# One block of 64-wide products a pair in place of two, set inside a unit of the MLP

## The chip, the core and the metric

The kernel runs on one core of a Trainium2 chip, in one launch. The core has a matrix engine (TensorE, PE in the profile; its weight loads are listed apart as PEld), three engines for elementwise work (VectorE or DVE, ScalarE or ACT, GpSimd or POOL) and a queue for transfers (SP). Products land in PSUM, a small accumulator memory of eight banks; each bank holds 512 fp32 numbers in each of 128 partitions. The metric is the device time of one execution in microseconds, smaller is better.

## The reference

Eight batches of eight heads go through retention (causal attention without softmax, with a decay of its own for each head), and the 4608 rows of 512 that come out go through an MLP with a leaky activation. All is fp32.

```python
# B, H, S, D = 8, 8, 576, 64;  d_model = 512, d_ff = 2048
scores = (q @ k.transpose(0, 1, 3, 2)) / sqrt(D)
gamma  = 1 - 2.0 ** (-5 - arange(H))
rel    = arange(S)[:, None] - arange(S)[None, :]
Dmat   = where(rel >= 0, gamma[:, None, None] ** rel, 0)
attn   = (scores * Dmat) @ v
x      = attn.transpose(0, 2, 1, 3).reshape(B * S, H * D)
h      = x @ w_in
out    = (max(h, 0) + alpha * min(h, 0)) @ w_out
```

## The kernel before

**Retention.** Two heads make a pair, so that a batch has four pairs and the whole 32. A sequence is cut into nine chunks of 64. Within a chunk the masked scores are used as they are; what came before a chunk comes in through running sums of k^T v, one 64x64 matrix a chunk, decayed from chunk to chunk. For a pair this takes three blocks of small products on TensorE: `ps` (scores of k and q in each chunk), `pu` (k^T v of each of the first eight chunks), and `pv` (values: scores times v and sums times q, in one product each).

```python
def pair_scores(n, kT, qT):                       # mt: masked scores and q, side by side
    ps = [ps_tile([P, NM, C], ...) for p2 in range(2)]        # two banks
    for j in range(NJ):                                        # nine chunks, two heads
        for h2 in range(2):
            x = (1 - h2, h2)[j % 2]
            nc.tensor.matmul(ps[j % 2][half(x), j // 2], kT[half(h2), chunk(j)],
                             qT[half(h2), chunk(j)], start=True, stop=True)
    for h2 in range(2):
        nc.scalar.copy(mt[half(h2), h2]..., qT[half(h2)])
    for p2 in range(2):                                        # four masks
        for h2 in range(2):
            nc.vector.scalar_tensor_tensor(out=mt[to, h2, p2::2], in0=ps[p2][half(x), 0:nm], ...)
    return mt

def pair_states(n, kn, vn):                       # su: running sums
    ps = [ps_tile([P, NM - 1, D], ...) for p2 in range(2)]    # two banks
    for j in range(NJ - 1):
        for h2 in range(2):
            nc.tensor.matmul(ps[j % 2][half(x), j // 2], kn[half(1 - h2), j],
                             vn[half(1 - h2), h2, j], start=True, stop=True)
    nc.scalar.copy(su[:, 0::2], ps[0])
    for h2 in range(2):
        nc.vector.scalar_tensor_tensor(out=su[half(h2), 1::2], ...)    # 2
    for j in range(3, NJ - 1, 2):
        nc.vector.scalar_tensor_tensor(out=su[:, j], ...)              # 3, each on the one before
    nc.vector.scalar_tensor_tensor(out=su[:, 2::2], ...)               # 1
    return su
def pair_sums(vn, su):                            # the sums go beside v
    for h2 in range(2):
        nc.scalar.copy(vn[half(h2), h2, 1:], su[half(h2)])
# ... pair_values(n, vn, mt): products of vn and mt into two banks, copied to xb
```

Each fp32 product in the code is two instructions on TensorE in the profile: 18 score products are 36 instructions, 16 of k^T v are 32. All these small products take their banks from one pool, `ps_a`, which has two.

**The MLP.** Rows are taken in token blocks of 256, and the work on one is cut into eight units. Both matrix products are done with seven products of half the size in place of eight; sums and differences make up for it. A unit computes 14 products into two banks `ph[0]` and `ph[1]` (three and four quarters of a bank; the fourth quarter of `ph[0]` is not used), brings them to `g` with ScalarE and VectorE, and hands `g` to the output products `po` of seven half-wide results in four banks. The output products of a unit are issued one unit later. After the eighth unit's output products, one ScalarE copy and seven sums on VectorE empty `po`. Banks are held once: `ph` of the next unit waits until this one's is read, and `po` of the next token block until the last one is emptied.

```python
def mlp_unit(kb, i):
    ph = [ps_h.tile([P, 4, P], ...) for m in range(2)]
    for n, (m, o, l, r) in enumerate(...):                     # 14 products (28 instructions)
        for cc in range(2):
            nc.tensor.matmul(ph[m][:, o], w_in[...][:, l, ...], r[:, cc], ...)
    nc.scalar.copy(g[:, 7], ph[0][:, 2])
    for o, x0, x1 in (...):                                    # 4 sums that read ph
        nc.vector.tensor_tensor(out=o, in0=x0, in1=x1, op=ALU.add)
    # ... then 2 tensor_scalar, 1 scalar_tensor_tensor and 4 tensor_tensor on g alone
    pend.append((kb, i, g))
    if len(pend) > 1:
        mlp_out()                                              # 7 products of the unit before;
                                                               # after unit 7: out_block (empties po)
```

**How both are laced.** From the third batch on (24 pairs), the units that are ready are shared out over a batch's four pairs, four to a pair in most batches, and each block of small products stands between two units:

```python
share = -(-len(queue) // (NPAIR - c))
cuts = [(share + i) // 3 for i in range(3)][::-1]
mt = pair_scores(n, kT, qT)                  # block ps
pop_units(cuts[0])
pair_sums(vn, pair_states(n, kn, vn))        # block pu
pop_units(cuts[1])
# ... scale and transpose the next pair's k and q
pair_values(n, vn, mt)                       # block pv
pop_units(cuts[2])
```

Instructions are put in order on each engine when the program is built: what is written first goes first, and where the next one would have to wait, a later one may be set ahead of it.

Of the kernel before, what the change touches and what calls it, by code (L numbers as in the profile page):

```python
# [10 lines left out]
FP32 = mybir.dt.float32  # L11
# [3 lines left out]
ALU = mybir.AluOpType  # L15
# [3 lines left out]
def kernel(  # L19
# [10 lines left out]
    nc = tc.nc  # L30
    B, H, S, D = q.shape
    NTOK, DM = out.shape
    DFF = moe_w_in.shape[1]
    P = 128

    NPAIR = H // 2
    C = 64
    NJ = S // C
    NM = (NJ + 1) // 2
# [21 lines left out]
    attn = ctx.enter_context(tc.tile_pool(name="attn", bufs=1))  # L61
# [5 lines left out]
    pairs = [(b, c) for b in range(B) for c in range(NPAIR)]  # L67

    def half(x):
        return slice(x * C, (x + 1) * C)  # L70
# [113 lines left out]
    mask = const.tile([P, C], FP32, name="mask")  # L184
# [262 lines left out]
                          (t[:, 2], b21, t[:, 1])):  # L447
            nc.gpsimd.tensor_tensor(out=o, in0=x0, in1=x1, op=ALU.subtract)  # L448

    def mlp_unit(kb, i):  # L450
        if kb not in xt:
            combine_x(kb)
        x, t = xb[kb], xt[kb]
        ph = [ps_h.tile([P, 4, P], FP32, tag=f"psh{m}", name=f"ph{m}_{kb}_{i}")
              for m in range(2)]

        for n, (m, o, l, r) in enumerate((
                (0, 2, 0, x[:, 0:2, 0:P]), (0, 0, 2, x[:, 2:4, 0:P]), (0, 1, 5, t[:, 1]),
                (1, 0, 4, t[:, 0]), (1, 1, 1, x[:, 0:2, P:TB]),
                (1, 2, 6, x[:, 2:4, P:TB]), (1, 3, 3, t[:, 2]))):  # L460
            for cc in range(2):
                nc.tensor.matmul(ph[m][:, o], w_in[i // UST][:, l, i % UST, cc], r[:, cc],  # L462
                                 start=(n in (0, 3) and cc == 0), stop=(n in (2, 6) and cc == 1),
                                 skip_group_check=True)


        g = mlp.tile([P, 8, P], FP32, tag="g", name=f"g_{kb}_{i}")
        nc.scalar.copy(g[:, 7], ph[0][:, 2])  # L468
        for o, x0, x1 in ((g[:, 0:5:4], ph[0][:, 0:2], g[:, 7:8].to_broadcast([P, 2, P])),
                          (g[:, 5:7], ph[1][:, 0:2], g[:, 4:5].to_broadcast([P, 2, P])),  # L470
                          (g[:, 3], ph[1][:, 0], g[:, 6]),
                          (g[:, 1:3], ph[1][:, 2:4], g[:, 5:7])):
            nc.vector.tensor_tensor(out=o, in0=x0, in1=x1, op=ALU.add)  # L473
        for m in range(2):
            fc = m * NU + i
            nc.vector.tensor_scalar(g[:, 4 + 2 * m:6 + 2 * m], g[:, 2 * m:2 * m + 2], 0.0,  # L476
                                    alpha[:, fc:fc + 1], ALU.min, ALU.mult)
        nc.vector.scalar_tensor_tensor(  # L478
            out=g[:, 0:4].rearrange("p x t -> p (x t)"),
            in0=g[:, 0:4].rearrange("p x t -> p (x t)"), scalar=0.0,  # L480
            in1=g[:, 4:8].rearrange("p x t -> p (x t)"), op0=ALU.max, op1=ALU.add)
        for o, x0, x1, op in ((4, 1, 3, ALU.add), (6, 0, 1, ALU.subtract),
                              (5, 4, 0, ALU.subtract), (7, 2, 5, ALU.subtract)):
            ins = nc.vector.tensor_tensor(out=g[:, o, :], in0=g[:, x0, :], in1=g[:, x1, :], op=op)  # L484

        combine(3, ins)
        assert i < NU - UST or not waiting
        pend.append((kb, i, g))
        if len(pend) > 1:
            mlp_out()  # L490
# [11 lines left out]
            if ready[kb] == b:  # L502
                queue.extend((kb, i) for i in range(NU))

    def pop_units(n):
        for _ in range(min(n, len(queue))):
            kb, i = queue.pop(0)
            mlp_unit(kb, i)
            if i == NU // 2 and kb + 1 < NKB and ready[kb + 1] <= done[0]:
                combine_x(kb + 1)  # L510

# [4 lines left out]
    def ps_tile(shape, name):  # L516
        return ps_a.tile(shape, FP32, tag="psa", name=name)
# [19 lines left out]
    def chunk(j):  # L537
        return slice(j * C, (j + 1) * C)
# [3 lines left out]
    def pair_scores(n, kT, qT):  # L542
        c = pairs[n][1]

        mt = attn.tile([P, 2 * S], FP32, tag="at", name=f"mt_{n}").rearrange(
            "p (h j s) -> p h j s", h=2, s=C)
        ps = [ps_tile([P, NM, C], f"ps{p2}_{n}") for p2 in range(2)]
        for j in range(NJ):
# [5 lines that stand above are left out]
            nc.scalar.copy(mt[half(h2), h2].rearrange("p j s -> p (j s)"), qT[half(h2)])  # L554
        for p2 in range(2):
            for h2 in range(2):
                h, to, x = 2 * c + h2, half(1 - h2), (1 - h2, h2)[p2]
                nm = NM - p2
                nc.vector.scalar_tensor_tensor(  # L559
                    out=mt[to, h2, p2::2], in0=ps[p2][half(x), 0:nm], scalar=th[to, 3, h:h + 1],  # L560
                    in1=mask[to, None, :].to_broadcast([C, nm, C]), op0=ALU.mult, op1=ALU.mult)
        return mt

    def pair_states(n, kn, vn):
        c = pairs[n][1]
        ps = [ps_tile([P, NM - 1, D], f"pu{p2}_{n}") for p2 in range(2)]
        for j in range(NJ - 1):
            for h2 in range(2):
                x = (h2, 1 - h2)[j % 2]
                nc.tensor.matmul(ps[j % 2][half(x), j // 2], kn[half(1 - h2), j],  # L570
                                 vn[half(1 - h2), h2, j], start=True, stop=True)
        su = attn.tile([P, S], FP32, tag="kT", name=f"su_{n}")[:, 0:S - D].rearrange(
            "p (j d) -> p j d", d=D)
        g1, g2 = gch[:, 0, c:c + 1], gch[:, 1, c:c + 1]
        nc.scalar.copy(su[:, 0::2], ps[0])
        for h2 in range(2):
            nc.vector.scalar_tensor_tensor(
                out=su[half(h2), 1::2], in0=su[half(h2), 0::2], scalar=g1[half(h2)],
                in1=ps[1][half(1 - h2)], op0=ALU.mult, op1=ALU.add)
        for j in range(3, NJ - 1, 2):  # L580
            nc.vector.scalar_tensor_tensor(out=su[:, j], in0=su[:, j - 2], scalar=g2,
                                           in1=su[:, j], op0=ALU.mult, op1=ALU.add)
        nc.vector.scalar_tensor_tensor(out=su[:, 2::2], in0=su[:, 1:NJ - 3:2], scalar=g1,  # L583
                                       in1=ps[0][:, 1:], op0=ALU.mult, op1=ALU.add)
        return su

    def pair_sums(vn, su):
        for h2 in range(2):
            nc.scalar.copy(vn[half(h2), h2, 1:], su[half(h2)])  # L589

    def pair_values(n, vn, mt):
        b, c = pairs[n]
        w = TB // C

        j1 = -b * NJ % w or w
        j1 += w if NJ - j1 > 6 else 0
        pv = [ps_tile([P, (j1, NJ - j1)[i], C], f"pv{i}_{n}") for i in range(2)]
        for j in range(NJ):
            for h2 in range(2):
                nc.tensor.matmul(pv[j >= j1][half(h2), j - (j1 if j >= j1 else 0)],  # L600
                                 vn[:, h2, j], mt[:, h2, j], start=True, stop=True)
        j = 0
        while j < NJ:
            kb, o = divmod(b * NJ + j, w)
            if kb not in xb:
                xb[kb] = ring.tile([P, NCC, TB], FP32, tag=f"x{kb % NRING}", name=f"xb_{kb}")
            m, i = min(w - o, NJ - j), j >= j1
            j0 = j - (j1 if i else 0)
            nc.scalar.copy(xb[kb][:, c, o * C:(o + m) * C].rearrange("p (j s) -> p j s", s=C),  # L609
                           pv[i][:, j0:j0 + m])  # L610
            j += m
# [274 lines left out]
    for n, (b, c) in enumerate(pairs):  # L886
        if n <= last:
            continue
        if n == last + 1:
            pop_units(1)  # L890
        if n + 1 < len(pairs) and n + 1 not in loaded:
            loaded[n + 1] = load_pair(n + 1)
        kn, _, _, vn = loaded[n]
        share = -(-len(queue) // (NPAIR - c))
        cuts = [(share + i) // 3 for i in range(3)][::-1]
        kT, qT = turned.pop(n)
        mt = pair_scores(n, kT, qT)
        pop_units(cuts[0])
        pair_sums(vn, pair_states(n, kn, vn))
        pop_units(cuts[1])  # L900
        if n + 1 < len(pairs):
            scale_pair(n + 1)
            turned[n + 1] = transposes(n + 1)
        pair_values(n, vn, mt)
        del loaded[n]
        pop_units(cuts[2])
        if c == NPAIR - 1:
            enqueue(b)
    pop_units(len(queue))
# [30 lines left out]
```

## Time and profile before

The time is 1026.29 us, the median of three runs (1025.18 to 1026.33).

| what | busy us | from |
|---|---|---|
| whole span | 1024.7 | head of the page |
| MLP units, first products (L462) | 277.8 + 213.4 | groups |
| MLP units, output products (L382) | 407.8 | groups |
| `pv` (L600), `ps` (L551), `pu` (L570) | 35.5, 22.3, 19.5 | groups |
| VectorE in all | 768.8 | engines |
| ScalarE in all | 267.5 | engines |
| transfers | 64.30 MB | DMA queues |

A group is named by its line in the kernel, its engine and what it writes and reads; "mean ns" is one instruction. Instructions of TensorE overlap, so a busy time of 218 ns for a small product says nothing of the step from one to the next; that is read from the starts in the trace. The chain of work that ended last lists, in order of time, on which instructions the end of the program hung: start, length, engine, name, line, number. A timeline lists all instructions of one engine, with the idle time ahead of them and who ended it in brackets.

### The profile page before, as it was taken

Reading aid. Unit: us, or ns where it says so; the run is one execution under the profiler, and the core shown is the slowest. Engines: PE = TensorE matmul, PEld = TensorE weight load, DVE = VectorE, ACT = ScalarE, POOL = GpSimd, SP = SyncE. Lnnn points to the kernel's source line nnn. Section 1 sums busy time; section 2 is a strip of 40 time slices with the busy share of each in tenths; the row PEclk is TensorE's granted clock in tenths of the full one; section 3 lists DMA queues with packets and bytes.
Section 4 is the critical chain, followed back from the end, with each engine's and each line's share of the span. In section 5 each row is a group of like instructions: output and inputs, shape, how many; then the busy total and the mean of one; then the engine's idle time right before and its main releaser. Section 6 shows DMA issues by size and latency. Waiting matters only on the chain.

```text
span 1024.7 us, 23101 instructions
## 1 busy us (share of the span) xinstructions
PE 1007.9 (98%) x9385; PEld 891.0 (87%) x9385; DVE 768.8 (75%) x2041; ACT 267.5 (26%) x599; POOL 176.7 (17%) x198
## 2 busy tenths in 40 slices
PE   6899999999999999999999999999999999999998
PEld 5666668999999999999999999999999999999997
DVE  7669967777878787776868787877787776667665
ACT  4556652223222222022122222222222211000000
POOL 4656675200200010100010000200020001010000
PEclk9999999999999999999999999999999999999999
DMA  9975744223223222112113222222222100000000
GB/s 237 234 195 146 184 75 97 46 59 59 62 42 67 49 46 57 24 45 45 41 31 67 47 52 46 63 46 59 48 47 57 24 22 2 22 1 21 1 21 22
DMA packets 229308, 64.30 MB, mean 63 GB/s; under 512 B 214337, under 2 KB 222545, under 8 KB 229201
## 3 DMA queue, kind: packets, MB, share of 16 engines
q1 hardware_dynamic: 227088, 62.29, 26.8%
q8 instruction: 74, 1.21, 0.5%
q10 hardware_dynamic: 2112, 0.53, 0.3%
q14 instruction: 34, 0.27, 0.1%
HBM read 53.35 MB, written 9.44 MB: 61 GB/s over the span
## 4 chain that ended last, share of the span: by engine, by line
PE 97%; DVE 1%; DMA 1%; ACT 0%; issue 0%; POOL 0%; ACTq 0%; DVEq 0%; POOLq 0%
PE ph L462 40%; PE po L382 38%; PE po L397 6%; PE ph L418 5%; PE pv L600 3%; PE ps L551 2%; PE pu L570 2%; DMA w_out<-in_q_dram 1%; PE pv L717 0%; PE pv L706 0%; PE ps L660 0%; DVE w_out L690 0%; PE pt L641 0%; DVE wc L308 0%; DVE pa L667 0%
## 5 line engine op out<-in xcount | busy, mean ns | idle before, releaser
L382 PE MATMUL po<-w_out,g 128*128 128x256 f32 x1792 | 407.8, 379 | 0.0
L382 PEld LDWEIGHTS po<-w_out,g 128*128 128x128 f32 x1792 | 331.1, 190 | 39.4
L473 DVE TENSOR_TENSOR g<-ph,g 128x256 f32<-128x256 f32 (+1 forms) x512 | 187.5, 387 | 184.9 <-ACT g L468 112.7
L462 PE MATMUL ph<-xb,w_in 128*128 128x128 f32 x2048 | 277.8, 279 | 0.0
L462 PEld LDWEIGHTS ph<-xb,w_in 128*128 128x128 f32 x2048 | 253.2, 192 | 8.1 <-issue 0.5
L462 PE MATMUL ph<-xt,w_in 128*128 128x128 f32 x1536 | 213.4, 275 | 0.0
L462 PEld LDWEIGHTS ph<-xt,w_in 128*128 128x128 f32 x1536 | 192.1, 192 | 0.0
L468 ACT COPY g<-ph 128x128 f32<-128x128 f32 x128 | 33.9, 265 | 395.7 <-PE ph L462 375.6
L484 DVE TENSOR_TENSOR g<-g 128x128 f32<-128x128 f32 x512 | 126.8, 289 | 7.8
L478 DVE SCALAR_TENSOR_TENSOR g<-g 128x512 f32<-128x512 f32 x128 | 91.7, 717 | 3.9
L476 DVE TENSOR_SCALAR g<-g,alpha 128x256 f32<-128x256 f32 x256 | 85.0, 374 | 3.7
L523 POOL TENSOR_TENSOR qx<-qx,tabx 128x576 f32<-128x576 f32 x28 | 32.7, 1167 | 310.9 <-DMA qx<-in_q_dram 255.0
L418 PE MATMUL ph<-xb,w_in 128*128 128x256 f32 x256 | 60.2, 390 | 1.4 <-ACT xb L724 1.4
L559 DVE SCALAR_TENSOR_TENSOR mt<-ps,th,mask 64x320 f32<-64x320 f32 (+1 forms) x112 | 57.8, 516 | 4.5 <-PE ps L551 2.7
L397 PE MATMUL po<-w_out,g 128*128 128x512 f32 x128 | 58.5, 599 | 0.9 <-DVE g L434 0.9
L418 PEld LDWEIGHTS ph<-xb,w_in 128*128 128x128 f32 x256 | 49.1, 195 | 11.1 <-issue 2.4
L448 POOL TENSOR_TENSOR xt<-xb 128x256 f32<-128x256 f32 x16 | 11.6, 726 | 214.4 <-PE ph L462 202.1
L448 POOL TENSOR_TENSOR xt<-xb,xt 128x256 f32<-128x256 f32 x32 | 23.6, 738 | 142.4 <-ACT xb L609 141.7
L528 ACT ACTIVATE vn<-vn,tabv 64x576 f32<-64x576 f32 x56 | 43.3, 773 | 16.2 <-DMA vn<-in_v_dram 15.7
L397 PEld LDWEIGHTS po<-w_out,g 128*128 128x128 f32 x128 | 23.5, 190 | 24.9 <-issue 22.5
L589 ACT COPY vn<-su 64x512 f32<-64x512 f32 x56 | 34.5, 616 | 37.5 <-DVE su L583 36.8
L609 ACT COPY xb<-pv 128x256 f32<-128x256 f32 (+3 forms) x84 | 22.6, 321 | 79.1 <-PE pv L600 79.1
(120 smaller groups left out, 687.0 us busy)
## 6 DMA issues: line engine op xcount, KB each, us to landing
out_dram<-osb SPq DMA_DIRECT2D x36, 256.0 KB, 2.3
kx<-in_k_dram SPq DMA_DIRECT2D x112, 72.0 KB, 2.8
qx<-in_q_dram SPq DMA_DIRECT2D x112, 72.0 KB, 2.5
vn<-in_v_dram SPq DMA_DIRECT2D x56, 144.0 KB, 3.2
kn<-in_k_dram SPq DMA_DIRECT2D x56, 144.0 KB, 3.2
raw<-in_moe_w_in_dram SPq DMA_DIRECT2D x24, 256.0 KB, 4.4
raw<-in_moe_w_out_dram SPq DMA_DIRECT2D x10, 512.0 KB, 4.3
w_in<-in_moe_w_out_dram SPq DMA_DIRECT2D x6, 512.0 KB, 5.4
```

The costliest lines, as they stand in the source:

```text
L382: nc.tensor.matmul(acc[kb][n // 2][:, n % 2, :], g[:, x, :], w_out[i][:, y, :], start=(i == 0 and n % 2 == 0), stop=(i == NU - 1 and (n % ...
L397: nc.tensor.matmul(acc[kb][m], g[:, 2 * x + m], w_out[i][:, 2 * x:2 * x + 2].rearrange("p x f -> p (x f)"), start=(i == 0 and x == 0), sto ...
L418: nc.tensor.matmul(ph[:, x], w_in[i // UST][:, cc // 2 * 2 + x, i % UST, cc % 2], xb[kb][:, cc], start=(cc == 0 and x == 0), stop=(cc == N ...
L448: nc.gpsimd.tensor_tensor(out=o, in0=x0, in1=x1, op=ALU.subtract)
L462: nc.tensor.matmul(ph[m][:, o], w_in[i // UST][:, l, i % UST, cc], r[:, cc], start=(n in (0, 3) and cc == 0), stop=(n in (2, 6) and cc == ...
L473: nc.vector.tensor_tensor(out=o, in0=x0, in1=x1, op=ALU.add)
L476: nc.vector.tensor_scalar(g[:, 4 + 2 * m:6 + 2 * m], g[:, 2 * m:2 * m + 2], 0.0, alpha[:, fc:fc + 1], ALU.min, ALU.mult)
L478: nc.vector.scalar_tensor_tensor(out=g[:, 0:4].rearrange("p x t -> p (x t)"), in0=g[:, 0:4].rearrange("p x t -> p (x t)"), scalar=0.0, in1 ...
L484: ins = nc.vector.tensor_tensor(out=g[:, o, :], in0=g[:, x0, :], in1=g[:, x1, :], op=op)
L528: nc.scalar.activation(vn[x, h2], vn[x, h2], ACTF.Copy, scale=tabv[x, c:c + 1])
L559: nc.vector.scalar_tensor_tensor(out=mt[to, h2, p2::2], in0=ps[p2][half(x), 0:nm], scalar=th[to, 3, h:h + 1], in1=mask[to, None, :].to_bro ...
L589: nc.scalar.copy(vn[half(h2), h2, 1:], su[half(h2)])
```

## The change

`ps` and `pu` of a pair become one block, and it stands inside the first unit of the pair's share: behind the unit's first products and ahead of the output products of the unit before. For this one of the two banks holds the results of the even chunks and the other those of the odd ones, of the first eight: scores in one half of the bank, k^T v in the other half. The ninth chunk's scores don't fit; they go into the free quarter of `ph[0]` of the unit around the block, and are masked first, so that this bank can be read and given back. The rest of the work on the block's results (copies, masks, running sums) is issued behind the unit's own work on `g`. Its purpose is that TensorE goes once and not twice a pair from full-size products to 64-wide ones and back. `pv` stays a block of its own between two units. The pairs of the first two batches, which run in a part with an order of its own, are as before. The unit count between the parts is changed too: one unit around the block, half of the share ahead of `pv`, the others behind it.

```diff
-    def mlp_unit(kb, i):
+    def mlp_unit(kb, i, front=None):
 ...(the 14 products into ph)
+        rest = front(ph[0][:, 3]) if front else None
         g = mlp.tile([P, 8, P], FP32, tag="g", name=f"g_{kb}_{i}")
 ...(the unit's work on g)
+        if rest:
+            rest()
         pend.append((kb, i, g))
         if len(pend) > 1:
             mlp_out()
 ...
+    def pair_front(n, kT, qT, kn, vn):
+        c = pairs[n][1]
+        mts[n] = mt = attn.tile([P, 2 * S], ...)
+        def products(extra):
+            ps = [ps_tile([P, 2, NM - 1, C], f"ps{p2}_{n}") for p2 in range(2)]
+            for j in (NJ - 1, *range(NJ - 1)):
+                for h2 in range(2):
+                    x = half((1 - h2, h2)[j % 2])
+                    nc.tensor.matmul(extra[x, 0:C] if j == NJ - 1 else ps[j % 2][x, 0, j // 2],
+                                     kT[half(h2), chunk(j)], qT[half(h2), chunk(j)],
+                                     start=True, stop=True, skip_group_check=True)
+            for j in range(NJ - 1):
+                for h2 in range(2):
+                    x = half((h2, 1 - h2)[j % 2])
+                    nc.tensor.matmul(ps[j % 2][x, 1, j // 2], kn[half(1 - h2), j],
+                                     vn[half(1 - h2), h2, j], start=True, stop=True,
+                                     skip_group_check=True)
+            for h2 in range(2):
+                to = half(1 - h2)
+                nc.vector.scalar_tensor_tensor(
+                    out=mt[to, h2, NJ - 1], in0=extra[to, 0:C],
+                    scalar=th[to, 3, 2 * c + h2:2 * c + h2 + 1], in1=mask[to],
+                    op0=ALU.mult, op1=ALU.mult)
+            def rest():
+                for h2 in range(2):
+                    nc.scalar.copy(mt[half(h2), h2].rearrange("p j s -> p (j s)"), qT[half(h2)])
+                for p2 in range(2):
+                    for h2 in range(2):
+                        ...(mask of eight chunks, as before)
+                pair_sums(vn, running_sums(n, ps[0][:, 1], ps[1][:, 1]))
+            return rest
+        return products
 ...
         share = -(-len(queue) // (NPAIR - c))
-        cuts = [(share + i) // 3 for i in range(3)][::-1]
-        kT, qT = turned.pop(n)
-        mt = pair_scores(n, kT, qT)
-        pop_units(cuts[0])
-        pair_sums(vn, pair_states(n, kn, vn))
-        pop_units(cuts[1])
+        assert share >= 3
+        pop_units(1, pair_front(n, *turned.pop(n), kn, vn))
+        pop_units(share // 2)
 ...(scale and transpose the next pair)
-        pair_values(n, vn, mt)
+        pair_values(n, vn, mts.pop(n))
         del loaded[n]
-        pop_units(cuts[2])
+        pop_units(share - 1 - share // 2)
```

`running_sums` is the second half of `pair_states`, unchanged, as a function of its own.

More of the change, by code (lines that the diff above doesn't have):

```diff
@@ L503, in enqueue, with pop_units @@
                 queue.extend((kb, i) for i in range(NU))
-    def pop_units(n):
+    def pop_units(n, front=None):
         for _ in range(min(n, len(queue))):
             kb, i = queue.pop(0)
-            mlp_unit(kb, i)
+            mlp_unit(kb, i, front)
             if i == NU // 2 and kb + 1 < NKB and ready[kb + 1] <= done[0]:
@@ L564, in pair_states @@
     def pair_states(n, kn, vn):
-        c = pairs[n][1]
         ps = [ps_tile([P, NM - 1, D], f"pu{p2}_{n}") for p2 in range(2)]
@@ L571, in pair_states, with running_sums @@
                                  vn[half(1 - h2), h2, j], start=True, stop=True)
+        return running_sums(n, *ps)
+    def running_sums(n, even, odd):
+        c = pairs[n][1]
         su = attn.tile([P, S], FP32, tag="kT", name=f"su_{n}")[:, 0:S - D].rearrange(
@@ L574, in pair_states @@
         g1, g2 = gch[:, 0, c:c + 1], gch[:, 1, c:c + 1]
-        nc.scalar.copy(su[:, 0::2], ps[0])
+        nc.scalar.copy(su[:, 0::2], even)
         for h2 in range(2):
@@ L578, in pair_states @@
                 out=su[half(h2), 1::2], in0=su[half(h2), 0::2], scalar=g1[half(h2)],
-                in1=ps[1][half(1 - h2)], op0=ALU.mult, op1=ALU.add)
+                in1=odd[half(1 - h2)], op0=ALU.mult, op1=ALU.add)
         for j in range(3, NJ - 1, 2):
@@ L583, in pair_states @@
         nc.vector.scalar_tensor_tensor(out=su[:, 2::2], in0=su[:, 1:NJ - 3:2], scalar=g1,
-                                       in1=ps[0][:, 1:], op0=ALU.mult, op1=ALU.add)
+                                       in1=even[:, 1:], op0=ALU.mult, op1=ALU.add)
         return su
@@ L589, in pair_sums @@
             nc.scalar.copy(vn[half(h2), h2, 1:], su[half(h2)])
+    def pair_front(n, kT, qT, kn, vn):
+        c = pairs[n][1]
+        mts[n] = mt = attn.tile([P, 2 * S], FP32, tag="at", name=f"mt_{n}").rearrange(
+            "p (h j s) -> p h j s", h=2, s=C)
+        assert C == D and NJ == 9
+        def products(extra):
[23 more added lines that the diff above has]
+                    for h2 in range(2):
+                        h, to, x = 2 * c + h2, half(1 - h2), (1 - h2, h2)[p2]
+                        nc.vector.scalar_tensor_tensor(
+                            out=mt[to, h2, p2:NJ - 1:2], in0=ps[p2][half(x), 0],
+                            scalar=th[to, 3, h:h + 1],
+                            in1=mask[to, None, :].to_broadcast([C, NM - 1, C]),
+                            op0=ALU.mult, op1=ALU.mult)
+                pair_sums(vn, running_sums(n, ps[0][:, 1], ps[1][:, 1]))
+            return rest
+        return products
     def pair_values(n, vn, mt):
```

## The prediction

> **What bounds the kernel now.** I read the page first, then the chain of work that ended last in order of time, then VectorE's timeline around one pair, then single start times in the trace.
>
> ```profile
> PE 1007.9 (98%) x9385; PEld 891.0 (87%) x9385; DVE 768.8 (75%) x2041; ACT 267.5 (26%) x599; POOL 176.7 (17%) x198
> PE 97%; DVE 1%; DMA 1%; ACT 0%; issue 0%; POOL 0%; ACTq 0%; DVEq 0%; POOLq 0%
> ```
>
> TensorE sets the end nearly everywhere. The next view, the chain over one pair of batch 5 (start, length, what), gives the price of each block of 64-wide products:
>
> ```profile
> 591.88 0.73 PE ps L551 x36
> 592.61 3.32 PE ph L462 x28
> 595.93 3.02 PE po L382 x14
> 598.96 3.12 PE ph L462 x28
> 602.08 3.02 PE po L382 x14
> 605.10 0.62 PE pu L570 x32
> 605.73 3.32 PE ph L462 x28
> 609.05 3.02 PE po L382 x14
> 612.08 1.20 PE pv L600 x36
> ```
>
> A unit of the MLP is 3.12 + 3.02 = 6.14 us without a wait. A unit behind a block has 3.32 instead of 3.12, so a block costs its own length and 0.20 more. Single starts from 160 us on show no longer gap between units: the change has no TensorE wait to take away, only these prices.
>
> VectorE is 75% busy over the span, and more around a pair: in 591.88 to 620.00 it is busy 22.64 of 28.12 us. Its timeline at a pair whose first unit is unit 0 of a token block:
>
> ```profile
> 592.58 2.11 DVE L559 SCALAR_TENSOR_TENSOR mt<-ps,th,mask 64x256 f32<-64x256 f32 x4 [0.17 <-PE ps L551]
> 594.72 0.42 DVE L473 TENSOR_TENSOR g<-ph,g 128x256 f32<-128x256 f32 x1
> ...
> 597.09 0.62 DVE L476 TENSOR_SCALAR g<-g,alpha 128x256 f32<-128x256 f32 x2
> 597.62 0.42 DVE L368 TENSOR_TENSOR osb<-po,s 128x256 f32<-128x256 f32 x1
> 597.95 0.68 DVE L478 SCALAR_TENSOR_TENSOR g<-g 128x512 f32<-128x512 f32 x1
> ...
> 600.68 0.42 DVE L368 TENSOR_TENSOR osb<-po,s 128x256 f32<-128x256 f32 x1
> 601.01 0.42 DVE L369 TENSOR_TENSOR osb<-po,u 128x256 f32<-128x256 f32 x1
> ...
> 606.17 0.98 DVE L577 SCALAR_TENSOR_TENSOR su<-su,gch,pu 64x256 f32<-64x256 f32 x2 [0.54 <-ACT su L575]
> 607.18 0.60 DVE L581 SCALAR_TENSOR_TENSOR su<-su,gch 128x64 f32<-128x64 f32 x2
> ```
>
> Two things are to be seen. Masked scores (mt), unit 0 (g) and the seven sums that empty the finished token block (osb) run back to back until 601.43, and TensorE begins the next block's output at 602.08. The pair's running sums (su) come only later, at 606.17. And the order is that of the program, except that one later instruction slips in where the next earlier one depends on the one just issued (597.62 between two g steps).
>
> **What the Trainium skill says.** "TensorEngine Tiling (Array Packing)", Key Properties: changing the tiling mode drains TensorE. The trace agrees: from the last output product to the first score is 309 ns (216 between units without a block), from the last score to the first full product 148, and then 214 to the second, where 111 is the cadence. "PSUM — Partial Sum Buffer", Engine vs sequencer instructions: the queues of ScalarE and VectorE are strictly first in, first out. The timeline agrees as far as it goes: nothing overtakes at run time, and what stands ahead in VectorE's queue delays the sums behind it. Same page, PSUM bank collisions: two engines must not touch one bank and 32-partition quadrant at once. The kernel before never puts products beside a unit's ph, so no run here shows yet what that costs; after the change ScalarE's copy and VectorE's first add of that bank must follow the two score products put in its free quarter.
>
> **The change, part by part.**
>
> 1. *Two blocks become one, 24 times* (pairs of batches 2 to 7). Price of a block, by starts, over the nominal step from one phase to the next: scores 309 + 580 + 148 + 214 - 328 = 923 ns (580 from first to last start, 328 = 216 + 112 nominal), sums 309 + 477 + 148 + 214 - 328 = 820 ns. Together 1743. The merged block has 68 products in 18 groups of four or two: the first step 106, sixteen steps of 58, some 20 within the last group, about 1059 ns. It is entered from ph, whose last product is 104 ns shorter than one of po (275 against 379): 309 - 104 = 205. It is left into po, whose cadence of 216 hides the weight load that cost 214 against 111. So 205 + 1059 + 148 - 112 = 1300. Saving 0.443 us a pair, **24 x 0.443 = 10.6 us**. No product is removed; pv keeps its block.
>
> 2. *VectorE gets a longer stretch in one unit.* Scores lose one chunk in each of two products-to-mask steps (549 - 482 = 67 ns, twice) and gain two small masks (about 284 each, the row of the 128x64 sums): +0.4 us a pair, beside TensorE. What matters is the place. Before, mask and sums lay two units apart; now both follow the same unit, and both stand in the program ahead of the emptying of po, because the rest is called before the output products.
>
> 3. *At unit 0 of a token block this collides.* Let 0 be the end of ph of the front unit A. TensorE: block to 1.29, output products of the old token block to 4.31, ph of the next unit to 7.43, then the output products of A. These overwrite po, bank by bank: the third bank is touched by the fifth pass, 4 x 0.432 later, at 9.16. VectorE can begin at about 0.45 (first products 0.20, their 0.22 and a semaphore). From then on, in program order: two small masks 0.56; unit A 4.03 (440.81 to 444.84 in another stretch of the timeline); masks 2.11; sums 2.15 (470.62 to 473.10 less a slipped-in 0.33); seven sums of po 2.33 (0.333 apart). Sum 11.18, so the last ends at 11.6 and the one that frees the third bank at 11.3. TensorE waits 11.3 - 9.16 = **2.1 us**. Before, the same instruction ended at 601.10, 5.2 on this clock (ph ended at 595.93), and the third bank was wanted at 7.9.
>
> 4. *How often.* Queues of 15, 16, 24, 16, 16 and 16 units are shared out over four pairs each; the chain confirms that the scores at 265, 321, 376, 536, 592, 647, 703, 758 and 814 us stand right before unit 0: nine. **9 x 2.1 = 18.9 us.**
>
> 5. *The other fifteen fronts.* Same sum without po: masks and sums are done by 9.3, or 10.6 if steps of unit B slip in; B's banks are wanted again at 10.45 and 11.8, and its g at 13.6, against some 13.0. They should just pass. The one pair with three units has its values one unit after the front, at 10.45, while the sums reach vn at about 11: +0.5 once.
>
> Sum: 1026.3 - 10.6 + 18.9 + 0.5 = 1035.1.
>
> **Rivals.** (a) *Only the saving shows*: 1026.3 - 10.6 = **1015.7**. For it: the kernel before has no wait on VectorE at all, ScalarE is idle three quarters of the time, and if more of the seven sums slip into the dependent steps of g and su, or if VectorE empties ph before the small masks, the third bank comes free earlier. Against it: the sum of work ahead of it, 11 us, doesn't depend on the order inside. (b) *VectorE's stretch also holds back the ordinary fronts*: with 1 us at each of the fifteen it is 1035 + 15 = **1050**. For it: margins of 0.6 us; against: the two-unit distance to the values. (c) *The bank shared with ph costs most*: copy and first add wait for products and small masks one after the other, 0.4 us more at each of the nine, **1039**.
>
> **Range and chances.** I hold the collision at unit 0 for likelier than not, two in three, with 1.4 to 2.5 us each: 1028 to 1039. One in three is rival (a) or something near. The point between them that I choose is 1032, pulled from 1035 toward the rival; the range runs from just above the full saving to (c): 1016 to 1041. More than 2% in either direction needs what I don't see: 1006 is twice the saving, 1047 is rival (b).
>
> **What would show it.** Right: in the chain, nine pieces of waiting on osb or s of L368 and L369, about 2 us each, just after the fronts at unit 0, with output products stretched from 3.02 to 5; one block of 68 products of about 1.2 us; the ph behind it gone back to 3.12. Step 1 wrong: the phase behind the merged block is longer by 0.2, or the block longer than 1.3. Step 3 wrong: no waits on VectorE, the sums of po standing ahead of su in its timeline. Rival (b): ph or po late behind every front. The whole prediction falls if the compiled order puts the emptying of po ahead of the rest.

## The result, and the profile after

The changed kernel takes 1053.13 us (median; 1052.34 to 1054.51), against 1026.33 for the kernel before in the same comparison: ratio **1.026**, interval 1.0246 to 1.0274. It is slower by 27 us, where the prediction chose 1032 and a range up to 1041.

First the page: the engines, and the chain that ended last.

```profile
PE 1014.4 (96%) x9385; PEld 898.4 (85%) x9385; DVE 782.0 (74%) x2089; ACT 267.4 (25%) x599; POOL 176.4 (17%) x198
PE 82%; DVE 12%; DMA 3%; ACT 2%; issue 1%; SPq 1%; DVEq 0%; POOL 0%; ACTq 0%
```

No engine has much more to do (VectorE 13 us more), but the chain runs over VectorE for 12% of the span where it was 1%. Six lines of the view of waits, longest first, name what stood in the way (engine, line, what it waited for; total us, times, longest):

```profile
POOL qx L527 <- DVE su L584: 199.4, 11, 29.7
ACT g L470 <- DVE mt L622: 140.9, 23, 8.6
DVE mt L622 <- PE ph L611: 61.2, 24, 2.9
PE po L382 <- DVE osb L368: 11.5, 9, 1.3
PE po L382 <- DVE u L368: 4.7, 8, 0.8
PE pv L653 <- ACT vn L596: 2.1, 10, 0.3
```

The fourth and fifth lines are the predicted wait, nine times: TensorE stands ahead of the output products of a new token block until VectorE has emptied the old one. The second and third are the chain through the bank of ph that is now shared; as waits of idle engines they cost nothing by themselves, but VectorE's work on g begins only behind them. The first and the last line I had not foreseen: GpSimd's work on the next pair's q now often starts just when VectorE has reached the pair's running sums, and pv waits for ScalarE.

TensorE's timeline at one of the nine fronts at unit 0 (front at 608.24):

```profile
615.24 0.61 PE L462 MATMUL ph<-xt,w_in 128*128 128x128 f32 x4
617.12 1.10 PE L382 MATMUL po<-w_out,g 128*128 128x256 f32 x4 [1.28 <-DVE osb L368]
618.62 1.13 PE L382 MATMUL po<-w_out,g 128*128 128x256 f32 x4 [0.40 <-DVE u L368]
619.69 0.61 PE L653 MATMUL pv<-mt,vn 128*64 128x64 f32 x8
620.49 0.34 PE L653 MATMUL pv<-mt,vn 128*64 128x64 f32 x4 [0.19 <-ACT vn L596]
620.75 1.56 PE L382 MATMUL po<-w_out,g 128*128 128x256 f32 x6
622.15 1.05 PE L462 MATMUL ph<-xb,w_in 128*128 128x128 f32 x8
```

Output products that take 3.02 us elsewhere spread from 617.12 to 622.15, and twelve instructions of pv stand in the middle of them. Presumably TensorE had nothing to do at this place when the program was put in order, so that the first values were set there; at run time they held up the six instructions behind them until ScalarE had written the sums into vn. VectorE's timeline over the same stretch shows why it is late:

```profile
608.62 0.58 DVE L622 SCALAR_TENSOR_TENSOR mt<-ph,th,mask 64x64 f32<-64x64 f32 x2 [2.91 <-PE ph L611]
609.59 0.42 DVE L475 TENSOR_TENSOR g<-ph,g 128x256 f32<-128x256 f32 x1 [0.39 <-ACT g L470]
609.93 0.77 DVE L538 STREAM_TRANSPOSE qT<-qx 128x576 f32<-128x576 f32 x1
610.62 0.39 DVE L475 TENSOR_TENSOR g<-ph,g 128x256 f32<-128x256 f32 x1
611.04 0.49 DVE L633 SCALAR_TENSOR_TENSOR mt<-ps,th,mask 64x256 f32<-64x256 f32 x1
...
616.04 0.48 DVE L584 SCALAR_TENSOR_TENSOR su<-su,gch,ps 64x256 f32<-64x256 f32 x1
616.55 0.42 DVE L368 TENSOR_TENSOR osb<-po,s 128x256 f32<-128x256 f32 x1
616.89 0.81 DVE L588 SCALAR_TENSOR_TENSOR su<-su,gch 128x64 f32<-128x64 f32 x1
...
617.97 0.27 DVE L588 SCALAR_TENSOR_TENSOR su<-su,gch 128x64 f32<-128x64 f32 x1
...
619.67 0.41 DVE L368 TENSOR_TENSOR osb<-po,s 128x256 f32<-128x256 f32 x1
```

The order is in the main the one that the prediction wrote down, but that steps of g, masks and sums alternate, and with one more instruction: the next pair's transpose, 0.77 us, right behind the first step of g. The first step itself comes at 609.59, 1.4 us after ph ended (608.15), because ScalarE's copy had to wait for the two small masks. The sum that frees the third bank of po (619.67) ends 11.9 us after ph's end, where the prediction had 11.3.

One thing is in neither the prediction nor the experiments below. Of the three small running sums (L588) the first takes 0.81 us and the others 0.27. Beside it GpSimd scales the next pair's q. At the last front at unit 0 (841.48) there is no such work, and no sum is long; the third bank is free 11.4 us after ph's end (GpSimd's timeline, then VectorE's at that last front):

```profile
616.48 1.15 POOL L527 TENSOR_TENSOR qx<-qx,tabx 128x576 f32<-128x576 f32 x1 [13.44 <-DMA qx<-in_q_dram]
```

```profile
850.13 0.28 DVE L588 SCALAR_TENSOR_TENSOR su<-su,gch 128x64 f32<-128x64 f32 x1
...
852.36 0.41 DVE L368 TENSOR_TENSOR osb<-po,s 128x256 f32<-128x256 f32 x1
```

GpSimd's scaling starts 8.2 to 9.1 us behind the front at the other eight fronts at unit 0, and each time one of the three sums takes 0.81 to 1.19 us. In the kernel before it started there too, but the sums stood later.

An ordinary front in the chain (start, length, what) looks as it should, but for the output products behind the block:

```profile
581.03 0.46 PE ps L611 x27
581.49 0.47 PE ps L617 x32
581.96 3.22 PE po L382 x14
585.18 3.12 PE ph L462 x28
588.30 3.02 PE po L382 x14
591.33 3.12 PE ph L462 x28
594.45 3.19 PE po L382 x14
```

They take 3.22 and not 3.02: behind a block, po pays the same 0.20 as ph did. And 594.45 shows a wait: 174 ns from the start of ph's last instruction to that of po's first, where 112 is the cadence, and then 320 to po's second, where 216 is, as g of the unit behind the front came late.

The bill, from front to next front (the same products lie between them before and after), in us more than before: nine fronts at unit 0 **+2.95** on average (2.30 to 3.22), twelve ordinary ones **-0.18**; the first +1.23, the one with three units +0.47. 9 x 2.95 - 12 x 0.18 + 1.23 + 0.47 = 26.1 of the 26.6 by which the profiled spans differ. The nine are not alike: the last one, without GpSimd, costs 2.30 and the other eight 3.03 on average, 0.72 more, where one sum takes 0.71 more. Of the twelve only the one without GpSimd beside its sums saves as much as 0.36.

### The profile page after: what moved, and what is told of

Read it like the earlier page. It is cut to its first block, busy times and chain, and to the rows that moved or that the text cites. A ratio compares the mean times of both kernels' runs of the same rounds, so it can differ in the third digit from the quotient of the medians.

```text
span 1051.3 us, 23049 instructions
## 1 busy us (share of the span) xinstructions
PE 1014.4 (96%) x9385; PEld 898.4 (85%) x9385; DVE 782.0 (74%) x2089; ACT 267.4 (25%) x599; POOL 176.4 (17%) x198
## 3 DMA queue, kind: packets, MB, share of 16 engines
q8 instruction: 74, 1.21, 0.5%
## 4 chain that ended last, share of the span: by engine, by line
PE 82%; DVE 12%; DMA 3%; ACT 2%; issue 1%; SPq 1%; DVEq 0%; POOL 0%; ACTq 0%
PE ph L462 34%; PE po L382 32%; PE po L397 5%; PE ph L418 5%; PE pv L653 3%; DVE mt L633 2%; DVE su L588 2%; ACT vn L596 1%; DVE g L475 1%; DMA w_out<-in_v_dram 1%; DVE su L584 1%; DMA raw<-in_moe_w_in_dram 1%; DVE g L486 1%; DVE g L480 1%; DVE qT L538 1%
## 5 line engine op out<-in xcount | busy, mean ns | idle before, releaser
L382 PE MATMUL po<-w_out,g 128*128 128x256 f32 x1792 | 416.7, 383 | 16.3 <-DVE osb L368 11.5
L382 PEld LDWEIGHTS po<-w_out,g 128*128 128x128 f32 x1792 | 329.1, 190 | 63.6 <-issue 12.9
L462 PE MATMUL ph<-xb,w_in 128*128 128x128 f32 x2048 | 272.7, 276 | 0.0
L462 PEld LDWEIGHTS ph<-xb,w_in 128*128 128x128 f32 x2048 | 257.1, 192 | 7.8 <-issue 0.7
L486 DVE TENSOR_TENSOR g<-g 128x128 f32<-128x128 f32 x512 | 130.2, 295 | 6.5
L622 DVE SCALAR_TENSOR_TENSOR mt<-ph,th,mask 64x64 f32<-64x64 f32 x48 | 13.6, 283 | 61.5 <-PE ph L611 61.2
L418 PEld LDWEIGHTS ph<-xb,w_in 128*128 128x128 f32 x256 | 49.3, 195 | 11.0 <-issue 2.4
L653 PEld LDWEIGHTS pv<-mt,vn 128*64 128x64 f32 x1008 | 35.8, 137 | 16.7 <-issue 11.6
L633 DVE SCALAR_TENSOR_TENSOR mt<-ps,th,mask 64x256 f32<-64x256 f32 x96 | 46.1, 480 | 2.3
```

The lines of the kernel that those rows point to most:

```text
L382: nc.tensor.matmul(acc[kb][n // 2][:, n % 2, :], g[:, x, :], w_out[i][:, y, :], start=(i == 0 and n % 2 == 0), stop=(i == NU - 1 and (n % ...
L418: nc.tensor.matmul(ph[:, x], w_in[i // UST][:, cc // 2 * 2 + x, i % UST, cc % 2], xb[kb][:, cc], start=(cc == 0 and x == 0), stop=(cc == N ...
L633: nc.vector.scalar_tensor_tensor(out=mt[to, h2, p2:NJ - 1:2], in0=ps[p2][half(x), 0], scalar=th[to, 3, h:h + 1], in1=mask[to, None, :].to_ ...
```

## Experiments

**Theory A:** what costs is the VectorE work that stands in its queue between a front and the next need for a bank that VectorE must empty; at unit 0 of a token block that work includes all of po. It says nothing of GpSimd, whose part I give where it changes what an experiment shows. **Rivals** are given with each experiment; the main one is that every front pays for the longer VectorE stretch, wherever it stands (R3). Times are compared by ratio to the kernel before on the same chip, which took 1024.9 us beside e1 to e4 and 1027.3 beside e5 to e8.

**e1: no values in the middle of po.**

```diff
+                # in pair_values, for each product: ordered behind the last product of po
+                tc.add_manual_dep(ins.ins, last_po[0].ins.name, <order only>)
```

> The changed kernel (1053.1) with one thing altered: the values' products are kept behind the output products that are written ahead of them, so that none of them stands in the middle of po at the nine fronts at unit 0. Theory A (two costs at unit 0: VectorE empties po too late, and the twelve early instructions of pv then hold the rest of po until ScalarE has copied the sums): about 0.7 us less at each of nine fronts, 1045 to 1048, and a wait of about 2.3 us left in po at each. Rival R1 (the early products only fill time that is lost to VectorE anyway): 1052 to 1054.

Measured: 1047.8, ratio 1.0224 (1.0209 to 1.0239). From front to front the nine lose 2.70 over before, 0.25 less than in the changed kernel. One of them is no fair comparison: from 279.7 us on e1 ran 3.4 us at a granted clock of 0.5, with output products 427 ns apart for 216. The other eight lose 2.56, 0.38 less than the same eight of the changed kernel, about half of what I gave the early values, 0.7: the rest of their time would have been lost to VectorE anyway, as R1 says. That the time lies in theory A's range is in part luck, as 1.9 us of the difference between the two traces lie ahead of the first front, where the kernels are alike. The last front at unit 0, without GpSimd and without early values, costs 1.93. TensorE's timeline at the front shown above (606.17 in e1) has a third wait where they stood:

```profile
615.06 1.10 PE L384 MATMUL po<-w_out,g 128*128 128x256 f32 x4 [1.28 <-DVE osb L368]
616.66 1.13 PE L384 MATMUL po<-w_out,g 128*128 128x256 f32 x4 [0.49 <-DVE u L368]
618.17 1.56 PE L384 MATMUL po<-w_out,g 128*128 128x256 f32 x6 [0.39 <-DVE osb L368]
```

**e2: po emptied ahead of masks and sums.**

```diff
-        if rest:
-            rest()
         pend.append((kb, i, g))
         if len(pend) > 1:
             mlp_out()
+        if rest:
+            rest()
```

> As e1, and the masks and running sums are written behind the output products and the emptying of po, no longer ahead of them. Theory A (what counts is how much VectorE work lies between the front and the next need for a bank): the wait leaves po and comes back in part at ph of the next unit, 1 to 1.5 us in place of 2.3 at each of the nine fronts: 1034 to 1040. Rival R2 (only the order was at fault): all nine waits gone, 1018 to 1024.

Measured: 1036.2, ratio 1.0111 (1.0094 to 1.0128). The nine fronts lose 1.08 in place of 2.70. The wait has moved to ph of the next unit but one, whose two banks VectorE now empties late:

```profile
607.51 3.19 PE L384 MATMUL po<-w_out,g 128*128 128x256 f32 x14
611.05 1.16 PE L465 MATMUL ph<-xb,w_in 128*128 128x128 f32 x8 [0.35 <-DVE g L478]
...
612.91 0.68 PE L465 MATMUL ph<-xt,w_in 128*128 128x128 f32 x4 [0.26 <-DVE g L478]
```

Theory A stands, R2 falls: this order gets back 1.6 us of each wait, but not all. Some of the 1.6 is GpSimd's, which no longer works beside the three sums here. Whether another order (this one with the small masks and the transposes late, say) would take all of the wait away at unit 0 is not tested.

**e3: fronts at other units.**

```diff
+        keep = 2 if 4 <= b < B - 1 else 0
-        share = -(-len(queue) // (NPAIR - c))
+        share = -(-(len(queue) - keep) // (NPAIR - c))
```

> The changed kernel with two units of each batch from the fifth on kept back for the next batch, so that the fronts stand at other units: four of them remain at unit 0 in place of nine. Nothing else is altered. Theory A (3.15 us between a front at unit 0 and another): 1053.1 - 5 x 3.15 = 1037 (1034 to 1041). Rival R3 (every front pays for VectorE's long stretch, wherever it stands): 1049 to 1054.

Measured: 1036.1, ratio 1.011 (1.0095 to 1.0126), within theory A's range; five fronts fewer at unit 0 give 15 us by ratio. R3 falls.

**e4: nothing of the block in a bank of ph** (the ninth chunk's scores are left out, the first chunk's stand in for them).

```diff
-            for j in (NJ - 1, *range(NJ - 1)):
+            for j in range(NJ - 1):
 ...
-                    out=mt[to, h2, NJ - 1], in0=extra[to, 0:C],      # ahead of g
+                    out=mt[to, h2, NJ - 1], in0=ps[0][to, 0, 0],     # in rest(), behind g
```

> As e1, and the ninth chunk's scores are left out of the block, so that nothing of it lies in a bank of ph; their two small masks stay but read the first chunk's scores, behind the unit's g (the ninth chunk's output is not the reference's). Theory A with the shared bank (ScalarE's copy of ph waits for the two small masks, which wait for the block's first products, 1 us before VectorE can start on g): about 0.9 us less at each of nine fronts and 0.12 us of products less at each of 24, against e1: 1033 to 1038. Rival R4 (the shared bank costs nothing, VectorE's sum of work alone counts): 1041 to 1045.

Measured: 1031.7, ratio 1.0064 (1.0049 to 1.0079): 16 us less than e1 by ratio, more than theory A gave (10 to 15). The nine lose 1.21 in place of 2.70, and the twelve ordinary fronts save 0.44 in place of 0.15. Of this, 0.12 a front are the products left out. The rest has two parts. One is VectorE's start on g: the small masks go behind g with the chain that led to it, and the first step comes 1.3 us before ph's end (596.79) and not 1.4 behind it:

```profile
595.50 0.42 DVE L478 TENSOR_TENSOR g<-ph,g 128x256 f32<-128x256 f32 x1 [1.15 <-ACT g L473]
```

The other is GpSimd, whose scaling does not meet the sums in e4. At the last front at unit 0, where it does not in e1 either, the cost falls from 1.93 to 1.20. So the shared bank with its early masks costs some 0.6 us there, less than theory A's 0.9. R4 falls.

**e5: the transposes held back** behind the running sums (order only), on top of e1.

> As e1, and VectorE's transposes of the next pair are kept behind the running sums, where in the changed kernel one of them (0.77 us) slips in between the first two steps of g at each front. Theory A (every VectorE instruction ahead of po's emptying lengthens the wait at unit 0 by its own length): 0.77 us less at each of nine fronts, 1040 to 1042. Rival R5 (the transpose fills a slot in which VectorE had to wait anyway): 1046 to 1049.

Measured: 1044.2, ratio 1.0162 (1.0147 to 1.0177), against e1 6.4 us less, where A gave 6.9. The agreement is luck. The nine fronts lose 2.19, the ordinary ones save 0.33. One wait of 0.99 and one of 0.38 are left in po:

```profile
612.21 2.09 PE L384 MATMUL po<-w_out,g 128*128 128x256 f32 x8 [0.99 <-DVE osb L368]
614.68 1.56 PE L384 MATMUL po<-w_out,g 128*128 128x256 f32 x6 [0.38 <-DVE osb L368]
```

The transpose held back frees the third bank of po 0.3 us sooner than at the last front of e1 (11.1 for 11.4 us after ph's end), not 0.77. At this front, where GpSimd did not meet the sums in e1, nothing is saved: 1.93 in e1, 2.19 in e5. What the other fronts gain goes with GpSimd: it no longer works beside the sums but at two fronts (the first and the one at 427 us), and outside unit 0 these two, with the three-unit one, are the only ones above -0.36 (1.24, -0.04 and -0.03). So the edit did not test the transpose alone, and R5 is not refuted.

**e6: the front in unit 1 where it fell on unit 0.**

```diff
+        lead = 1 if queue[0][1] == 0 else 0
+        pop_units(lead)
         pop_units(1, pair_front(n, *turned.pop(n), kn, vn))
         pop_units(share // 2)
 ...
-        pop_units(share - 1 - share // 2)
+        pop_units(share - 1 - lead - share // 2)
```

> The changed kernel, but where a pair's first unit is unit 0 of a token block, that unit is issued first and the front goes into unit 1; nothing else is altered, and no unit is moved to another pair. Theory A (at unit 1 the emptying of po lies ahead of the front in VectorE's queue, so that no front collides): all 24 fronts cost what the fifteen others do in the changed kernel, -0.2 us a pair on average and 1 to 2 us in all for the first and the three-unit pair: 1021 to 1024 against 1024.9 of before. Rival R3 (the work piles up one unit later and is paid there): above 1030.

Measured: 1024.0 against 1027.3, ratio **0.9968** (0.9956 to 0.9979). Nine fronts put one unit later, and 30 us of the changed kernel's time are gone by ratio; in TensorE's waits no line with po and VectorE's emptying is left. R3 falls a second time.

**e7: as e6, and the small masks behind the four sums that read ph.**

```diff
         for o, x0, x1 in (...):
             nc.vector.tensor_tensor(out=o, in0=x0, in1=x1, op=ALU.add)
+        if small:
+            small()            # the two small masks, taken out of products()
```

> As e6, and the two small masks of the ninth chunk are written behind the four sums that read ph, no longer ahead of ScalarE's copy of it. Theory A with the shared bank (unit A's g comes 0.9 us late because copy, small masks and first products follow one another; that is what is left as waits of 0.1 to 0.2 us at the ordinary fronts): these waits go and each pair saves the 0.34 us that the starts in the trace give: 1016.5 to 1019. Rival R4 (the bank sharing isn't what makes the ordinary fronts late): as e6.

Measured: 1020.3 against 1027.3, ratio **0.993** (0.9915 to 0.9945), 3.9 us better than e6 by ratio (3.0 in the traces from the first front to the last): better than both kernels. The absolute figure lies above the range I gave, which was worked out from 1024.9 and not from the 1027.3 of this chip; the saving is 7.0 us against before, and 24 x 0.36 less what the trace shows lost at the first pair (1.6), the one with three units (0.6) and one other (0.3) is 6.1. The chain from a front in unit 1 to just before the next pair's front:

```profile
598.41 0.47 PE ps L619 x32
598.89 3.22 PE po L382 x14
602.11 3.12 PE ph L462 x28
605.23 3.02 PE po L382 x14
608.26 3.12 PE ph L462 x28
611.38 3.02 PE po L382 x14
614.40 1.20 PE pv L656 x36
615.60 3.32 PE ph L462 x28
```

Every phase is back at 3.12 and 3.02, but for the two behind a block. From front to front over two pairs, such a stretch is 0.72 us shorter than before, **0.36 a pair**: the merge's gain without any wait.

But this does not show that the small masks made the ordinary fronts late. With the edit two other things moved: the transpose, from 1.7 us behind each front to 7.7, and GpSimd's scaling, which no longer meets the sums. Two of the sums in e6, then in e7:

```profile
609.98 1.57 DVE L588 SCALAR_TENSOR_TENSOR su<-su,gch 128x64 f32<-128x64 f32 x2
```

```profile
606.57 0.59 DVE L590 SCALAR_TENSOR_TENSOR su<-su,gch 128x64 f32<-128x64 f32 x2
```

The two last stretches from front to front, where GpSimd has nothing to scale, are alike in e6 and e7 to 0.01 us, with the small masks early or late; and e5 brings eleven of its twelve ordinary fronts to -0.36 with the small masks early. So R4's mechanism stands, although its time does not, and GpSimd beside the sums is the likelier cause of the late g.

**e8: e7 with the transposes held back.**

> As e7, and the transposes are kept behind the running sums as in e5. Theory A: what is left of the waits goes, above all at the first pair: 1016 to 1018, a saving of 24 x 0.34 = 8.2 us against before. Rival: as e7 within 0.5 us, since no front waits for VectorE any more there.

Measured: 1021.1 against 1027.3, ratio 0.9939 (0.9922 to 0.9955), not told apart from e7, as the rival had it. Theory A's extra gain at the first pair isn't there: that front costs 1.09 over before (1.24 in e7), so the transpose is not its main cause. GpSimd is the likely one: it works on the weights beside the three sums there, which take 2.1 us more than elsewhere in e8 and 1.8 in e7. No run moved this work alone.

## Why the prediction was wrong

*Mechanism and count: right.* Step 4's nine fronts at unit 0 are the nine that lose, and step 3's wait stands where it was put, at po of the front's own unit, released by osb and u; it is spread over po's first three banks, with 1.28 us ahead of the first. e3 and e6 show that the place of the front decides.

*Step 1, "a saving of 0.443 us a pair": too large.* The entry, 205 ns, and the block are as worked out (1046 for 1059, whose parts add up to 1054; exit 148). Wrong was that po's cadence "hides the weight load": from the first to the second output product behind a block it is 320 ns and not 216. Without it the saving is 0.34; e7 shows 0.36, and 24 x 0.36 = 8.6 for 10.6.

*Step 3, "Sum 11.18, so the last ends at 11.6": the step that failed, in its term "sums 2.15".* Against a front without waits (-0.36), one at unit 0 costs 2.95 + 0.36 = 3.3 us in place of 2.1. Where nothing else comes in, at the last front of e1, it is 1.93 + 0.36 = 2.3, and the third bank is free at 11.4 for the predicted 11.3. That this is so near is luck: the transpose and the 0.39 us in which VectorE waits for ScalarE's copy were left out, and apparently masks that fill gaps between dependent steps of g make up for them. Two things come on top. At eight of the nine fronts one of the running sums takes 0.71 us more while GpSimd scales the next q, so that "sums 2.15" is some 2.9; I had measured it in the kernel before, at a place where GpSimd stood still. And the values set into po cost 0.38 (e1). Together 2.3 + 0.38 + 8/9 x 0.72 = 3.3, nine times: 9 x 1.2 = 11 us more than predicted. For the values e1 is an experiment; for GpSimd there is the comparison of fronts within the traces, but no run that moved its scaling alone. Rival (c), the shared bank, is part of the 2.3: e4 puts it at some 0.6.

*Step 5, "They should just pass": not quite.* The ordinary fronts lose 0.18 of the 0.36 through g that comes late, nearly all of them beside a sum that GpSimd lengthens; the first and the three-unit front lose 1.6 and 0.8 against -0.36. Rival (b), 1 us at each, was too strong, but it wasn't zero: 12 x 0.18 + 1.6 + 0.8 = 4.6 us.

*The choice of 1032.* The sum was 1035.1, and I pulled it toward rival (a) because more of po's emptying might slip forward. It slips (616.55, 617.63), but it frees the third bank no earlier, since the last sums come at the end of the same queue. With the sizes read from the traces: 1026.3 - 8.6 + 9 x 3.3 + 4.6 = 1052, which is bookkeeping and no test.

*What the Trainium skill gave.* "TensorEngine Tiling (Array Packing)", Key Properties, was right in kind: each change of mode has its price, here 0.20 in the chain behind the block for ph and po alike. The bank rule of "PSUM — Partial Sum Buffer", PSUM bank collisions, shows as a chain: ScalarE's copy of one quarter of the bank waits for VectorE's masks of another (23 waits at the changed kernel's 24 fronts). It costs some 0.6 us where po is waiting (e4); that it costs anything at an ordinary front is not shown.

## What to carry to other kernels

Fewer mode changes on a full TensorE are worth what the starts in the trace say (0.36 us a pair here), and such a sum is spoilt by one wait of some microseconds on an engine that is only three quarters busy: before moving work, add up what stands in that engine's queue between the new place and the next need for a buffer it has to empty, with everything that can slip in, every engine that alternates with it and every engine that works beside it, at each phase of the loop. A duration measured where GpSimd stands still need not hold where it works. If one phase in four or eight collides, move the block by one unit there before giving up the merge. A free corner of a bank isn't free while another engine reads that bank: here the unit's own work on g started 2.7 us later than in e4, which leaves the corner empty.

## What the runs showed of the hardware

Sixty-eight instructions of 64-wide products, each a 64x64 tile of the array, start 58 ns apart in groups of four and don't slow down when two kinds of them follow each other: 1046 ns from the first to the last. The delay between the first and the second full-size product after a block is 104 ns over the cadence for products of 256 columns (320 for 216) as for those of 128 (214 for 111). It is not peculiar to a change of mode: where po starts late with no block ahead of it, as at 594.35 of the changed kernel, the first two are 320 ns apart as well.

Some of VectorE's instructions take longer beside GpSimd. In the changed kernel between 160 and 900 us a small sum (su from su and gch, 128x64) takes 276 ns on average without GpSimd (47 of them) and 929 with it (25), a step of g from g alone (128x128) 286 and 598. Those of g and osb that read PSUM show no such difference: 415 and 420 for g from ph (128x256), 415 and 424 for osb.
